# Window attention beside a Fourier mix: sums of v in bursts of four blocks instead of three

## The chip, the cores and the metric

The kernel runs on one core of a Trainium2 chip. A core has a matrix engine (TensorE, PE in the profile, with its weight loads as PEld), a vector engine (VectorE, DVE), an activation engine (ScalarE, ACT), a general engine (GpSimd, POOL) and a queue engine (SyncE, SP) that here only issues transfers. Each engine runs its own instructions in their order and waits on semaphores for the others. The metric is the device time of one execution in microseconds (us); lower is better. Several executions are timed, and one more is recorded by the profiler.

## The reference

Two mixers of the same x (2048 rows of 512) are blended row by row by a gate:

```python
g = _sigmoid((x * gate_w).sum(-1, keepdims=True))
a = einsum("ts,bse->bte", dft_seq_re, x @ dft_hid_re.T) - einsum("ts,bse->bte", dft_seq_im, x @ dft_hid_im.T)
# b: 32 heads of 16, window of 256
scores = jnp.einsum("bhqd,bhkd->bhqk", q, k) * (Dh ** -0.5)
mask = (idx[:, None] - idx[None, :] >= 0) & (idx[:, None] - idx[None, :] < W)
p = _softmax(jnp.where(mask[None, None], scores, -1e9), axis=-1)
b = jnp.einsum("bhqk,bhkd->bhqd", p, v) (heads side by side) @ wo
return g * a + (1 - g) * b
```

a is a discrete Fourier transform written as dense matrix products; b is causal attention in which a row sees itself and the 255 rows before it. B_x is not used: both mixers take A_x.

## The kernel before

**The dense work.** Products in float32 are made of three products of a high and a low part each (TERMS). All dense work of the projections and of the transform (tiles dqk, dv, dab, dc, lines 244, 266, 446; 128x512 each) is one generator, `stream`, that yields after nearly every matmul. The big part is dc: 1536 matmuls, blocks of 48. Its matrices cr and ci come in pieces through the tile raw, and DVE splits each piece in a high part (L80) and a low part (L81).

**The attention.** 2048 rows are 32 blocks of 64; 32 heads are four groups of eight, so there are 128 blocks (N), group after group. A pair is two heads; a group has four pairs (p = 0 to 3). Scores are computed twice. First, `s_pair(n, p)` computes the scores of the 64 queries of block n against up to 320 keys (PE, L325), DVE adds the mask and takes the row minimum (L327), and ACT takes the exponential and the row sum (L330). After each eight blocks `ml_rows` turns minima and sums into rows (a reciprocal and three copies on DVE, two small matmuls L337, three stores through SP), and two visits later `m_ring` sends the minima's rows into the ring buffer of the queries, by a transfer on ACT's queue. Second, LAG = 20 visits behind, `t_pair(k, p)` computes the transposed scores of the 64 keys of block k against up to 320 queries (PE, L388), ACT takes the exponential into the tile pt (L389), and after every second pair POOL zeroes the corners outside the window by four selects (L394, L398; two where the sequence ends). pt has four buffers, a whole block each.

**The sums of v.** `pv(j)` multiplies block j's pt with v (tile vpad, L415): matmuls with 32 columns of weights, so that the four pairs lie beside each other in the array, summed in the PSUM tile o. A tile o holds 512 queries; where a block's window crosses into the next 512, the block's sums are two pieces. When eight blocks have ended, DVE multiplies o with the reciprocal row sums (L425), which a transfer has brought, and the result is stored (o_scr). vpad is made by `v_spread` for four blocks at once (two copies on POOL, L378) from the tile vr that `v_load` fetches; vpad has two buffers and vr one.

**The order.** PE runs in the order written by hand. The loop over visits n does, for each quarter p: one s tile of block n, some matmuls of the stream (`fill`), one T tile of block k = n - 20, another fill. A fill gives 1.5 to 1.8 matmuls on average. The tiles of s, T and ml_rows take turns in four PSUM buffers (pool ps_a, tag st). `make_pad` prepares the stationary operands (two buffers each, on DVE and ACT). At the end of the third quarter of every third visit, PE runs a burst: the sums of the last three blocks, one block after another, and behind it `ml_rows` when a set of eight blocks is due. The other engines' order is set by a planner that simulates the program.

**Behind the loop.** `attention_done` (L640) loads wo. The rest of the stream follows: `wo_prep` reads o_scr back and splits it (tile os), `wo_block` multiplies with wo (L669, 12 matmuls a block), in groups between blocks of dc.

Of the kernel before, what the change touches and what calls it, by code (L numbers as in the profile page):

```python
# [25 lines left out]
LAG = 20  # L26
# [6 lines left out]
def fnet_window_mix(ctx: ExitStack, tc: tile.TileContext, xT, x, wqk, wv, wr, wi, cr, ci, wo, gw, out):  # L33
# [21 lines left out]
    def ld(dst, src):  # L55
        mark("sp", nc.sync.dma_start(dst, src))

    def f(ap):
        return ap.bitcast(F32)
# [7 lines left out]
    @contextmanager  # L67
    def behind(*engines):
        with ExitStack() as es:
            for e in engines:  # L70
                if e in last:
                    es.enter_context(tc.issue_after(last[e]))
            yield
# [98 lines left out]
    def clear_rows(i, ss):  # L172
        nc.gpsimd.memset(f(ring[i][96:128, :, ss * 512:(ss + 1) * 512]), 0.0)
# [7 lines left out]
    def clear_pads():  # L181
        for t in vpad:
            nc.gpsimd.memset(t, 0.0)
        for t in pads[1]:
            nc.gpsimd.memset(f(t[96:128]), 1.0)
            for h in range(2):
                a = t[96:128, :, 64 * h:64 * h + 64]
                nc.vector.tensor_scalar(a, f(a), mrow[96:128, h:h + 1], None, op0=OP.mult)
# [110 lines left out]
    def make_pad(i, n):  # L299
        if not 0 <= n < NG * NB:  # L300
            return
        t = pads[i][n % NPAD]
        b = n % NB
        with behind(*(("act", "dve") if n < NPAD else ())):
            for h in range(2):
                src, dst = f(ring[i][:96, :, b * BQ:(b + 1) * BQ]), t[:96, :, 64 * h:64 * h + 64]
                if i and h:
                    nc.scalar.activation(dst, src, AF.Copy, scale=half[:96, h:h + 1])  # L308
                else:
                    nc.vector.tensor_scalar(dst, src, half[:96, h:h + 1], None, op0=OP.mult)  # L310
        PAD[i, n] = t
# [21 lines left out]
    def ml_rows(u):  # L333
        ml = ML.pop(u)
        nc.vector.reciprocal(ml[:, 1], ml[:, 1])
        pt = ps_a.tile([P, 512], F32, name="s", tag="st")
        nc.tensor.matmul(pt[:64, :P], ml.rearrange("p x c -> p (x c)"), ident, start=True, stop=True)  # L337
        hl = at.tile([32, 2, 2, 64], F32R, name="mhl", bufs=1)
        m = pt[:32, :P].rearrange("c (a r) -> c a r", a=2)
        nc.vector.tensor_scalar(hl[:, :, 0], m, -1.0, None, op0=OP.mult)  # L340
        nc.vector.scalar_tensor_tensor(hl[:, :, 1], m, -1.0, f(hl[:, :, 0]), op0=OP.mult, op1=OP.subtract)
        ld(m_scr[u].rearrange("x p (j r) -> (p j) x r", r=64), f(hl[:]).rearrange("c a h r -> c (a h) r"))
        lt = at.tile([64, P], F32, name="lt", bufs=1)
        nc.vector.tensor_copy(lt[32:64], pt[32:64, :P])
        for a in range(2):
            ls = l_scr[u]
            ld(bass.AP(tensor=ls.tensor, offset=ls.offset + a * 512, ap=[[1024, NP], [64, 8], [1, 64]]),
               lt[32:64, 64 * a:64 * a + 64])

    def m_ring(u):  # L350
        U = u % 4
        with behind("act"):
            nc.scalar.dma_start(f(ring[0][96:100, :, U * 512:(U + 1) * 512]), m_scr[u])
# [17 lines left out]
    def v_spread(n):  # L371
        if n >= NG * NB:
            return
        raw = VR.pop(n)
        v2 = vpad[n // 4 % 2]
        for h in range(2):
            r = slice(64 * h, 64 * h + 64)
            nc.gpsimd.tensor_copy(v2[r, :, :, 16 * h:16 * h + 16], raw[r].rearrange("r j (p d) -> r j p d", d=16))  # L378
        V2[n // 4] = v2

    def t_pair(n, p):
        q0 = n % NB * BQ
        w = min(WIN, S - q0)
        if p == 0:
            PT[n] = at.tile([P, NP, WIN], F32, name="pt", bufs=4)
        pt = PT[n]
        ps = ps_a.tile([P, 512], F32, name="t", tag="st")
        nc.tensor.matmul(ps[:, :w], PAD[1, n][:, p], ring[0][:, p, q0:q0 + w], start=True, stop=True)  # L388
        nc.scalar.activation(pt[:, p, :w], ps[:, :w], AF.Exp, scale=-1.0)  # L389
        if p % 2:  # L390
            ph = slice(p - 1, p + 1)
            for h in (0, 64):
                a = pt[h:h + 64, ph, 0:64]
                nc.gpsimd.affine_select(a, a, pattern=[[0, 2], [1, 64]], compare_op=OP.is_ge, fill=0.0,  # L394
                                        base=0, channel_multiplier=-1)
                if w == WIN:
                    a = pt[h:h + 64, ph, 256:320]
                    nc.gpsimd.affine_select(a, a, pattern=[[0, 2], [-1, 64]], compare_op=OP.is_gt, fill=0.0,  # L398
                                            base=0, channel_multiplier=1)

    def pv(n):
        g, kb = divmod(n, NB)
        v2 = V2[n // 4][:, n % 4]
        pt = PT.pop(n)
        q0 = kb * BQ
        w = min(WIN, S - q0)
        q = q0
        while q < q0 + w:
            sb = q // 512
            e = min(q0 + w, (sb + 1) * 512)  # L410
            first = (g, sb) not in OT
            if first:
                OT[g, sb] = ps_o.tile([P, 512], F32, name="o")
            for p in range(NP):
                nc.tensor.matmul(OT[g, sb][32 * p:32 * p + 32, q - sb * 512:e - sb * 512], v2[:, p],  # L415
                                 pt[:, p, q - q0:e - q0], start=first, stop=kb == 8 * sb + 7,
                                 skip_group_check=True)
            q = e
        if kb % 8 == 7:
            sb = kb // 8  # L420
            ps = OT.pop((g, sb))
            rl = ev.tile([P, 512], F32, name="ev")
            ls = l_scr[g * 4 + sb]
            ld(rl, bass.AP(tensor=ls.tensor, offset=ls.offset, ap=[[512, 2 * NP], [0, 16], [1, 512]]))
            nc.vector.tensor_mul(rl, ps, rl)  # L425
            ld(o_scr[sb][g], rl)
# [251 lines left out]
    def need(key):  # L678
        while key not in have:
            next(stream)  # L680
# [3 lines left out]
    def ring_ahead(n):  # L684
        nonlocal loaded
        while loaded < 16:
            g, ss = divmod(loaded, 4)
            if n >= 32 * g + 8 * ss:
                need(("qk", g, ss))
            if ("qk", g, ss) not in have or n - LAG < 32 * (g - 1) + 8 * ss + 9:  # L690
                break
            with behind(*(("sp",) if g == 0 else ())):
                ring_load(g, ss)
            loaded += 1

    def fill(n):
        nonlocal quota
        rate = FILL_FIRST if n < LAG else FILL_SEQ if "proj" in have else FILL_PROJ
        quota += rate / 2
        while quota >= 1:  # L700
            next(stream, None)
            quota -= 1

    ctx.enter_context(tc.manual_schedule(engines={mybir.EngineType.PE}))
    N = NG * NB
    maxima = sent = 0
    taken = []
# [1 line left out]
    ring_ahead(0)  # L709
    need(("v", 5))  # L710

    for n in range(N + LAG + 2):
        if n in (1, 3, 5):
            for i in range(2):
                clear_rows(1 - i, (n + 1) // 2)
        if n == 7:
            clear_pads()
        k = n - LAG
        ring_ahead(n + 1)
        if -4 <= k < N - 4 and k % 4 == 0:  # L720
            for c in range(2):
                need(("v", (k + 4) % NB // 2 + c))
            with behind(*(("sp",) if k < 4 else ())):
                v_load(k + 4)
        if -4 <= k and k % 4 == 3:
            v_spread(k + 1)
        if n == 0:
            make_pad(0, 0)
        for p in range(NP):
            if n < N:  # L730
                s_pair(n, p)
            fill(n)
            if 0 <= k < N:
                t_pair(k, p)
            if p == 0:
                make_pad(0, n + 1)
                if k >= -1:
                    make_pad(1, k + 1)
            fill(n)
            if p == 2 and sent < maxima and n >= taken[sent] + 2:  # L740
                m_ring(sent)
                sent += 1
            if p == 2 and k % 3 == 0:
                for j in range(k - 3, k):
                    if 0 <= j < N:
                        pv(j)
                if maxima < 16 and n > 8 * maxima + 8:
                    ml_rows(maxima)
                    maxima += 1
                    taken.append(n)  # L750
    attention_done()
    for _ in stream:
        pass
# [44 lines left out]
```

## Time and profile before

| | |
|---|---|
| time, median of 3 runs | 871.07 us (869.48 to 871.13) |
| profiled execution, own time | 873.39 us |
| its span, first to last instruction | 871.3 us |
| PE busy | 860.5 us, 99% |
| DVE busy | 611.3 us, 70% |
| ACT busy | 580.9 us, 67% |
| POOL busy | 384.6 us, 44% |

Busy is the time in which an engine had at least one instruction at work, as a share of the span. Matmuls overlap: the next starts before the one before has ended, and so the distance between two starts, not the duration of one, tells what a matmul costs PE. In a row of the timeline the columns are the start in us, the duration in us, the engine, the line, the operation, the tiles (written <- read), the shape and how many instructions are merged; in brackets the idle time before it and who ended it. In a row of the waits, an engine and the tile it works on stand left of the arrow, and who was waited for right of it, then the total in us, how often, and the longest in us.

### The profile page before, as it was taken

How to read it: one execution, taken by the hardware profiler on the slowest of the kernel's cores; microseconds unless marked ns; L12 is line 12 of the kernel's file. 1: busy time of each engine (PE TensorE's matmuls, PEld its weight loads, DVE VectorE, ACT ScalarE, POOL GpSimd, SP SyncE). 2: the span in 40 equal slices, each digit the busy share in tenths (PEclk: the TensorE clock that was granted, in tenths of full speed). 3: DMA queues.
4: the chain of work that ended last, by engine and by line, in shares of the span. 5: the costliest groups of instructions: out<-in, count | busy, mean ns of one | idle time of the engine just before them, and what ended most of it. 6: DMA issues, size and time to landing. Idle time of an engine off the chain costs nothing.

```text
span 871.3 us, 17146 instructions
## 1 busy us (share of the span) xinstructions
PE 860.5 (99%) x5160; PEld 690.3 (79%) x5160; DVE 611.3 (70%) x1974; ACT 580.9 (67%) x1793; POOL 384.6 (44%) x1067
## 2 busy tenths in 40 slices
PE   8999999999999999999999999999999999999998
PEld 6888778787877778878788887878778787788886
DVE  4588987667878987878787777788876444564431
ACT  4388799888897987878788777877776454111110
POOL 9100054545444756656456566554546665200000
PEclk9999999999999999999999999999999999999999
DMA  6875796464749436644445354599944333485541
GB/s 229 266 226 155 248 262 197 153 214 158 241 158 289 130 105 225 172 130 135 134 131 170 105 163 133 156 349 256 329 148 159 123 118 114 130 263 192 189 145 48
DMA packets 93132, 157.87 MB, mean 181 GB/s; under 512 B 27120, under 2 KB 36080, under 8 KB 93040
## 3 DMA queue, kind: packets, MB, share of 16 engines
q1 hardware_dynamic: 92288, 155.61, 56.5%
q10 hardware_dynamic: 752, 1.18, 0.4%
q8 instruction: 40, 0.66, 0.3%
q14 instruction: 52, 0.43, 0.2%
HBM read 106.69 MB, written 50.07 MB: 180 GB/s over the span
## 4 chain that ended last, share of the span: by engine, by line
PE 92%; DVE 3%; DMA 2%; ACT 1%; issue 1%; SPq 0%; DVEq 0%; ACTq 0%
PE dc L446 40%; PE dab L266 9%; PE s L325 8%; PE o L415 8%; PE dqk L244 8%; PE t L388 8%; PE t L669 5%; PE dv L266 4%; DVE sm L327 1%; PE s L232 1%; DMA raw<-x 1%; ACT sm L330 1%; DMA ring<-qk_scr 1%; PE s L337 1%; DMA pt<-xT 0%
## 5 line engine op out<-in xcount | busy, mean ns | idle before, releaser
L446 PE MATMUL dc<-big,hi 128*128 128x512 f32 x1024 | 355.4, 395 | 0.0
L394 POOL TENSOR_SCALAR_AFFINE_SELECT pt<-pt 64x128 f32<-64x128 f32 x512 | 191.9, 375 | 276.4 <-ACT pt L389 261.2
L330 ACT ACTIVATE sm<-sm,ml 128x320 f32<-128x320 f32 (+4 forms) x512 | 277.3, 543 | 49.4 <-DVE ml L327 48.0
L327 DVE CUSTOM_DVE_ANT_0 sm<-s,mask 128x320 f32<-128x320 f32 (+4 forms) x512 | 230.7, 462 | 82.7 <-PE s L325 62.5
L389 ACT ACTIVATE pt<-t 128x320 f32<-128x320 f32 (+4 forms) x512 | 208.7, 412 | 89.8 <-PE t L388 86.2
L446 PEld LDWEIGHTS dc<-big,hi 128*128 128x128 f32 x1024 | 186.3, 188 | 32.6 <-issue 2.4
L446 PE MATMUL dc<-big,lo 128*128 128x512 f32 x512 | 201.6, 394 | 0.0
L398 POOL TENSOR_SCALAR_AFFINE_SELECT pt<-pt 64x128 f32<-64x128 f32 x448 | 161.9, 361 | 0.1
L325 PE MATMUL s<-ring,pad 128*128 128x320 f32 (+4 forms) x512 | 159.0, 310 | 0.9 <-DVE ml L327 0.5
L388 PE MATMUL t<-ring,pad 128*128 128x320 f32 (+4 forms) x512 | 155.1, 303 | 1.6 <-DVE ml L327 0.9
L310 DVE TENSOR_SCALAR pad<-ring,half 96x256 fp32r<-96x256 f32 x384 | 121.6, 358 | 24.2 <-PE t L388 22.0
L325 PEld LDWEIGHTS s<-ring,pad 128*128 128x128 f32 x512 | 96.0, 188 | 36.6 <-issue 7.4
L388 PEld LDWEIGHTS t<-ring,pad 128*128 128x128 f32 x512 | 96.1, 188 | 21.6 <-DVE ml L327 2.6
L446 PEld LDWEIGHTS dc<-big,lo 128*128 128x128 f32 x512 | 96.3, 188 | 10.6
L81 DVE TENSOR_TENSOR lo<-raw,hi 128x512 fp32r<-128x512 f32 x146 | 99.6, 712 | 1.4 <-PE dc L446 1.3
L330 ACT ACTIVATION_READ_ACCUMULATOR sm<-sm,ml 128x1 f32 x512 | 98.8, 193 | 0.0
L266 PE MATMUL dab<-hi,big 128*128 128x512 f32 x256 | 90.9, 396 | 0.0
L244 PE MATMUL dqk<-big,hi 128*128 128x512 f32 x240 | 86.7, 394 | 0.6 <-DVE hl L86 0.5
L80 DVE CAST hi<-raw 128x512 fp32r<-128x512 f32 x142 | 58.6, 453 | 38.3 <-PE dc L446 37.1
L415 PE MATMUL o<-pt,vpad 128*32 128x320 f32 (+4 forms) x1408 | 73.8, 351 | 0.0
L378 POOL COPY vpad<-vr 64x256 f32<-64x256 f32 x64 | 26.0, 405 | 91.1 <-DMA vr<-v_scr 72.0
L308 ACT ACTIVATE pad<-ring,half 96x256 fp32r<-96x256 f32 x128 | 64.1, 500 | 0.0
(82 smaller groups left out, 780.3 us busy)
## 6 DMA issues: line engine op xcount, KB each, us to landing
qk_scr<-hl SPq DMA_DIRECT2D x32, 512.0 KB
ring<-qk_scr SPq DMA_DIRECT2D x32, 512.0 KB
raw<-cr SPq DMA_DIRECT2D x32, 512.0 KB
raw<-ci SPq DMA_DIRECT2D x32, 512.0 KB
ab_scr<-hl SPq DMA_DIRECT2D x20, 512.0 KB
big<-ab_scr SPq DMA_DIRECT2D x20, 512.0 KB
r_scr<-ev SPq DMA_DIRECT2D x36, 256.0 KB
ev<-r_scr SPq DMA_DIRECT2D x36, 256.0 KB
```

The costliest lines, as they stand in the source:

```text
L244: nc.tensor.matmul(ps, w[a][:, c:c + 128], XT[dk, ss][:, b], start=n == 0, stop=n == 11)
L266: nc.tensor.matmul(ps, XT[dk, ss][:, a, c * 128:(c + 1) * 128], wh[b], start=n == 0, stop=n == 11)
L310: nc.vector.tensor_scalar(dst, src, half[:96, h:h + 1], None, op0=OP.mult)
L325: nc.tensor.matmul(ps[:, :w], PAD[0, n][:, p], ring[1][:, p, k0:k0 + w], start=True, stop=True)
L327: mark("dve", nc.vector.tensor_tensor_reduce(out=sm[:, :w], in0=ps[:, :w], in1=mask[:, WIN - w:], scale=1.0, scalar=3e38, op0=OP.add, op1= ...
L330: mark("act", nc.scalar.activation(sm[:, :w], sm[:, :w], AF.Exp, bias=nm[:, c], scale=-1.0, accum_out=l[:, c]))
L388: nc.tensor.matmul(ps[:, :w], PAD[1, n][:, p], ring[0][:, p, q0:q0 + w], start=True, stop=True)
L389: nc.scalar.activation(pt[:, p, :w], ps[:, :w], AF.Exp, scale=-1.0)
L394: nc.gpsimd.affine_select(a, a, pattern=[[0, 2], [1, 64]], compare_op=OP.is_ge, fill=0.0, base=0, channel_multiplier=-1)
L398: nc.gpsimd.affine_select(a, a, pattern=[[0, 2], [-1, 64]], compare_op=OP.is_gt, fill=0.0, base=0, channel_multiplier=1)
L415: nc.tensor.matmul(OT[g, sb][32 * p:32 * p + 32, q - sb * 512:e - sb * 512], v2[:, p], pt[:, p, q - q0:e - q0], start=first, stop=kb == 8 ...
L446: nc.tensor.matmul(ps, w[a][:, i % 8 * 128:i % 8 * 128 + 128], ab[SC[i]][:, b], start=i == ends[0] and a + b == 0, stop=i == ends[1] and a ...
```

## The change

- The sums of v run for four blocks, in the second quarter of every visit with k divisible by four: behind that quarter's s tile and its first fill. They cover blocks k-4 to k-1. `ml_rows` moves with them.
- In these visits (k > 0) the T tiles of block k are not one per quarter: the first quarter has none, the second has pair 0 (behind the burst), the third pair 1, the fourth pairs 2 and 3, one directly behind the other.
- `v_spread` for the next four blocks runs in visits with k % 4 == 2 instead of 3.
- The loop has one visit fewer: 149 instead of 150. The last burst (blocks 124 to 127) is in the last visit, where before the last one summed two blocks.

```diff
-    for n in range(N + LAG + 2):
+    for n in range(N + LAG + 1):
...
-        if -4 <= k and k % 4 == 3:
-            v_spread(k + 1)
+        if -4 <= k and k % 4 == 2:
+            v_spread(k + 2)
         if n == 0:
             make_pad(0, 0)
+        sums = k > 0 and k % 4 == 0
         for p in range(NP):
             if n < N:
                 s_pair(n, p)
             fill(n)
+            if k % 4 == 0 and p == 1:
+                for j in range(k - 4, k):
+                    if j >= 0:
+                        pv(j)
+                if maxima < 16 and n > 8 * maxima + 8:
+                    ml_rows(maxima)
+                    maxima += 1
+                    taken.append(n)
             if 0 <= k < N:
-                t_pair(k, p)
+                for q in ((), (0,), (1,), (2, 3))[p] if sums else (p,):
+                    t_pair(k, q)
...
-            if p == 2 and k % 3 == 0:
-                for j in range(k - 3, k):
-                    if 0 <= j < N:
-                        pv(j)
-                if maxima < 16 and n > 8 * maxima + 8:
-                    ml_rows(maxima)
-                    maxima += 1
-                    taken.append(n)
```

## The prediction

> **What bounds the kernel now.** I read the page first, then the busy time of the loop's stretch, then the order of TensorE (PE) around a burst of sums, then the waits of PE's weight loads, then POOL's masks, and last the chain of waits behind the loop.
>
> ```profile
> PE 860.5 (99%) x5160; PEld 690.3 (79%) x5160; DVE 611.3 (70%) x1974; ACT 580.9 (67%) x1793; POOL 384.6 (44%) x1067
> ...
> PE 92%; DVE 3%; DMA 2%; ACT 1%; issue 1%; SPq 0%; DVEq 0%; ACTq 0%
> ```
>
> ```profile
> core 0: us, PE busy (x) PEld busy (x) DVE busy (x) ACT busy (x) POOL busy (x), PEclk, DMA share, GB/s
> 123.40:758.90 635.50, 633.15 (x4152) 504.41 (x4151) 470.37 (x1574) 485.37 (x1524) 351.64 (x1000) 1.00 0.55 174
> ```
>
> PE carries 92% of the chain that ended last; in the stretch with bursts it is busy 633.15 of 635.50 us at a clock of 1.00, ACT 485.37 (76%) and DVE 470.37 (74%). So a change helps only if it takes time out of PE's own queue, and it hurts if it makes PE wait. A busy PE hides slots in which matmuls stand further apart than they need to. These show around a burst:
>
> ```profile
> 663.98 0.31 PE L388 MATMUL t<-ring,pad 128*128 128x320 f32 x1
> 664.13 0.39 PE L446 MATMUL dc<-big,hi 128*128 128x512 f32 x1
> 664.45 1.82 PE L415 MATMUL o<-pt,vpad 128*32 128x320 f32 x24
> 666.20 0.50 PE L446 MATMUL dc<-big,hi 128*128 128x512 f32 x1
> 666.53 0.39 PE L446 MATMUL dc<-big,lo 128*128 128x512 f32 x1
> ```
>
> ```profile
> 757.76 0.39 PE L446 MATMUL dc<-big,lo 128*128 128x512 f32 x1
> 757.99 0.39 PE L446 MATMUL dc<-big,hi 128*128 128x512 f32 x1
> 758.30 0.54 PE L415 MATMUL o<-pt,vpad 128*32 128x128 f32 x16
> 758.77 0.50 PE L446 MATMUL dc<-big,hi 128*128 128x512 f32 x1
> 759.11 0.40 PE L446 MATMUL dc<-big,lo 128*128 128x512 f32 x1
> ```
>
> Starts tell the slots: a dc matmul takes 757.99 - 757.76 = 0.23 us, a 320-column tile of T (or s) 664.13 - 663.98 = 0.15. The first burst sums three blocks of 320 columns (960), the second the last two blocks of a group, cut by the end of the sequence to 128 and 64 columns (192). From the dc before to the second dc behind it, the first takes 666.53 - 664.13 = 2.40 us, the second 759.11 - 757.99 = 1.12. So a column costs (2.40 - 1.12)/768 = 1.667 ns (a block 0.53 us), and what stays over is 1.12 - 0.32 - 2 x 0.23 = 0.34 us: a fixed price of each burst, split between the gap ahead of it (0.31 instead of 0.23) and the first matmul behind it (0.34 instead of 0.23).
>
> **The change, part by part.**
>
> *Fewer bursts.* Before, a burst comes at every third visit (k = 3 to 129: 43). After, at every fourth (k = 4 to 128: 32). The columns summed are the same. Eleven fixed prices go: 11 x 0.34 = -3.7 us. All of it lies in PE's queue, on the path. ml_rows stands right behind a burst in both, so its two small matmuls keep their place; one visit fewer in the loop only moves some 14 fill matmuls behind the loop, at the same 0.23.
>
> *The sums visit.* One visit (four quarters, each with an s tile, a T tile and two fills) is read from s tiles ten quarters apart:
>
> ```profile
> 527.18 0.30 PE L325 MATMUL s<-ring,pad 128*128 128x320 f32 x1
> ...
> 538.42 0.31 PE L325 MATMUL s<-ring,pad 128*128 128x320 f32 x1
> ```
>
> A quarter is 11.24/10 = 1.12 us, so a fill is (1.12 - 2 x 0.15)/2 = 0.41. s and T tiles share four PSUM buffers: a tile must be read by DVE (s) or ACT (T) before the fourth one after it starts. Ordinarily that leaves two quarters, 2.24 us. With two T tiles in the last quarter, four handovers per sums visit have three fills and four tiles: 3 x 0.41 + 4 x 0.15 = 1.83 us. Missed handovers in the kernel before:
>
> ```profile
> PEld s L325 <- ACT sm L330: 3.6, 7, 0.5
> PEld s L325 <- DVE ml L327: 3.3, 9, 0.6
> ...
> PEld t L388 <- DVE ml L327: 2.6, 6, 0.8
> ...
> PEld s L325 <- ACT pt L389: 2.0, 4, 0.8
> PEld o L415 <- POOL pt L398: 1.6, 5, 0.4
> ```
>
> The first four rows: 26 misses, 11.5 us, 0.44 each, among 1024 tiles. The change makes 4 x 31 = 124 of them shorter by 0.41. Low end: 0, or a gain of a few misses, because ACT and DVE catch up during a longer burst just ahead. High end: each of the 31 visits misses one, 31 x 0.44 = 13.6. I take one miss, +0.4, near the low end, because the tight handovers come directly behind a burst, when both engines' queues are empty, and 26 in 1024 are missed at all.
>
> *Masks.* The last block's T pairs must be exponentiated (ACT) and masked by four selects (POOL) before the burst reads them. From that block's last T tile to its own products there were a tile, a fill, three quarters and two blocks: 0.56 + 3.36 + 1.07 = 5.0 us. After it is three tiles, four fills and three blocks: 0.45 + 1.64 + 1.60 = 3.7. The time needed, from the tile's start to the end of the fourth select, is mostly below that, but not always:
>
> ```profile
> 278.30 0.31 PE L388 MATMUL t<-ring,pad 128*128 128x320 f32 x1
> ```
>
> ```profile
> 281.83 0.30 POOL L398 TENSOR_SCALAR_AFFINE_SELECT pt<-pt 64x128 f32<-64x128 f32 x1
> ```
>
> ```profile
> 469.56 0.31 PE L388 MATMUL t<-ring,pad 128*128 128x320 f32 x1
> ```
>
> ```profile
> 470.99 1.02 POOL L394 TENSOR_SCALAR_AFFINE_SELECT pt<-pt 64x128 f32<-64x128 f32 x1 [0.88 <-ACT pt L389]
> 471.98 0.29 POOL L398 TENSOR_SCALAR_AFFINE_SELECT pt<-pt 64x128 f32<-64x128 f32 x1
> 472.31 1.32 POOL L394 TENSOR_SCALAR_AFFINE_SELECT pt<-pt 64x128 f32<-64x128 f32 x1
> 473.59 0.29 POOL L398 TENSOR_SCALAR_AFFINE_SELECT pt<-pt 64x128 f32<-64x128 f32 x1
> ```
>
> ```profile
> 573.39 0.31 PE L388 MATMUL t<-ring,pad 128*128 128x320 f32 x1
> ```
>
> ```profile
> 577.23 0.30 POOL L398 TENSOR_SCALAR_AFFINE_SELECT pt<-pt 64x128 f32<-64x128 f32 x1
> ```
>
> Of the 124 blocks behind the start, ten need more than 3.7: the first is the tile at 278.30 (3.83), the last that at 573.39 (4.14), one of the worst that at 469.56 (473.88 - 469.56 = 4.32). Their excess sums to 3.6 us over 124 blocks; 31 of these now stand at the end of a burst: 3.6 x 31/124 = +0.9. Low end 0, high end 31 x 0.62 = 19 (each as late as the tile at 469.56). I take +0.9.
>
> In the late case two selects take 1.02 and 1.32 instead of 0.29, while DVE splits a piece:
>
> ```profile
> 472.20 0.68 DVE L81 TENSOR_TENSOR lo<-raw,hi 128x512 fp32r<-128x512 f32 x1
> ```
>
> [...]
>
> *v_spread, a visit earlier.* Its two copies on POOL move away from the visit whose masks the burst awaits, and their wait for a burst goes:
>
> ```profile
> POOL vpad L378 <- PE o L415: 16.6, 18, 1.7
> ```
>
> After, the buffer's last burst lies two visits back. The 16.6 us were POOL's idle time, on no path; gain 0 to the masks' 0.9, taken as 0. Its load keeps its place and has two visits (9 us) to land instead of three; SP's later loads wait on it no longer than before.
>
> *ml_rows, pv's load and product, m_ring.* DVE now has the product with 1/l and the three ml copies behind one burst in every second sums visit, ahead of the third s tile; SP gets their stores in another order. They stand where DVE has just idled: 0, with the handovers' upper end covering them. The ring rows sent by m_ring are read seven quarters and a burst later (7 x 1.12 + 2.5 = 10.3 us); no PE wait on such a transfer shows before: 0.
>
> *Behind the loop.* The output blocks now start after 64 dc matmuls instead of 92, in five groups instead of four.
>
> ```profile
> 758.84 21.12 PE dc L446 x92
> ```
>
> ```profile
> 773.56 0.68 DVE L81 TENSOR_TENSOR os<-ev,os 128x512 fp32r<-128x512 f32 x1
> ```
>
> Before, the first group's operands were ready at 774.2, 15.4 us into the 21.12. After, there are 64 x 0.23 = 14.7 us. At most 0.7 short, but the first group's three reads now stand on SP ahead of the store of the last burst, so 0.
>
> **Sum.** -3.7 + 0.4 + 0.9 = -2.4 us. The profiled execution took 873.39 us (span 871.3), 2.3 above the median of 871.07; I take the difference to the median: 868.7. What measurement can tell from no change is about 0.2%, 1.7 us.
>
> **Rivals.**
> 1. *Handovers (slower).* For it: ACT and DVE are at 76 and 74%, and the two T tiles arrive together. Against: the misses above are few. At one miss in every second sums visit, 16 x 0.44 = 7.0: -3.7 + 0.9 + 7.0 = +4.2, 875.3. It turns the result slower by 0.2% from (1.7 + 2.8)/0.44 = 10 more misses. Chance 0.14.
> 2. *Masks late (slower).* By the contention in the row at 472.20: if a split meets the last masks in every third burst, 10 x 0.62 = 6.2: -3.7 + 0.4 + 6.2 = +2.9, 874.0. For it: 1.3 us less reserve. Against: v_spread no longer delays that visit. Chance 0.07.
> 3. *Eaten up (same).* Both in part, 3 us together: -0.7, 870.4. Chance 0.18.
> 4. *The whole gain and more (faster).* No new wait, and a few old misses go: -4.5, 866.6. Chance 0.13.
> My forecast (866.9 to 869.3) has 0.48. Faster 0.61, same 0.18, slower 0.21. The range 865.5 to 873.5 leaves out most of the first two rivals; its low end is the saving with some four misses gone.
>
> **What would show it.** 32 bursts, each with the 0.34; PE's time between loop start and end shorter by 11 of them. Waits of PEld on POOL around 1 us in total say the masks were sized right, 6 or more say rival 2; the four handover rows near 12 us in total say the forecast, near 19 rival 1. A gap ahead of the first output group would show the stage behind the loop wrong. A fixed price that grows with the blocks in a burst would make the first term wrong.

## The result: slower by 0.7%

The changed kernel takes 876.23 us (median of 6 runs, 873.9 to 878.95), the kernel before beside it 870.11 us (6 runs, 868.44 to 871.13). The ratio is 1.0071 with a 95% interval of 1.0048 to 1.0095. The prediction was 868.7; its range ended at 873.5. The profiled execution took 877.35 us with a span of 875.5 us. The six runs of the changed kernel differ in PE's mean granted clock: the run of 873.9 has 1.000, those of 877.35 to 878.95 have 0.996 or 0.997.

The page of the changed kernel, its busy time and the engines' shares of the chain that ended last:

```profile
PE 860.7 (98%) x5160; PEld 693.1 (79%) x5160; DVE 610.7 (70%) x1974; ACT 582.3 (67%) x1793; POOL 386.5 (44%) x1067
...
PE 76%; DMA 4%; ACT 2%; DVE 2%; issue 1%; POOL 1%; ACTq 0%; SPq 0%; DVEq 0%; POOLq 0%
```

The windows view of the changed kernel over the same stretch of 635.5 us as in the prediction:

```profile
123.40:758.90 635.50, 626.50 (x4105) 501.07 (x4098) 467.87 (x1561) 484.41 (x1515) 350.82 (x991) 1.00 0.55 173
```

PE carried 92% of the chain before and carries 76% after; DMA doubled to 4%. The two shares of PE don't compare as they stand: both are shares of the whole span, and the chain of the changed kernel is followed back only to 122.99 us, over 86% of it; of that part PE has 88%. The stretch is the better measure. There PE stands still for 635.50 - 626.50 = 9.0 us, where it was 2.35. So the kernel lost time in waits of PE, and more of the chain runs through transfers.

**The bursts.** A burst of four blocks in PE's timeline of the changed kernel (start, duration):

```profile
666.02 0.39 PE L446 MATMUL dc<-big,lo 128*128 128x512 f32 x1
666.25 0.61 PE L446 MATMUL dc<-big,hi 128*128 128x512 f32 x2
666.80 2.39 PE L415 MATMUL o<-pt,vpad 128*32 128x320 f32 x32
669.11 0.42 PE L388 MATMUL t<-ring,pad 128*128 128x320 f32 x1
669.37 0.40 PE L446 MATMUL dc<-big,lo 128*128 128x512 f32 x1
```

From 666.02 to 669.37 are 3.35 us: three dc slots (0.69), one T slot (0.15), 1280 columns at 1.667 ns (2.13), and 0.38 over, with the rounding of six slots in it. The same reckoning over all 32 bursts, late masks left out, gives 0.35 to 0.36 for each of the 18 without `ml_rows`. The 14 with `ml_rows` stand at 0.73 each, because its two small matmuls are counted in. That makes 16.8 us for all; the 43 bursts before, again 14 of them with `ml_rows`, took 20.5. The difference is -3.7 us, as predicted.

**Late masks.** PE's timeline around the burst at 122.28, then POOL's and DVE's at the same place:

```profile
122.28 2.35 PE L415 MATMUL o<-pt,vpad 128*32 128x320 f32 x28
125.01 0.73 PE L415 MATMUL o<-pt,vpad 128*32 128x320 f32 x4 [0.39 <-POOL pt L398]
```

```profile
122.23 0.77 POOL L394 TENSOR_SCALAR_AFFINE_SELECT pt<-pt 64x128 f32<-64x128 f32 x1 [0.85 <-ACT pt L389]
122.95 1.05 POOL L398 TENSOR_SCALAR_AFFINE_SELECT pt<-pt 64x128 f32<-64x128 f32 x1
124.05 0.65 POOL L394 TENSOR_SCALAR_AFFINE_SELECT pt<-pt 64x128 f32<-64x128 f32 x1
124.66 0.29 POOL L398 TENSOR_SCALAR_AFFINE_SELECT pt<-pt 64x128 f32<-64x128 f32 x1
```

```profile
122.82 0.72 DVE L81 TENSOR_TENSOR lo<-raw,hi 128x512 fp32r<-128x512 f32 x1
...
123.87 0.68 DVE L81 TENSOR_TENSOR lo<-raw,hi 128x512 fp32r<-128x512 f32 x1
```

The four selects end at 124.95, and the burst's last matmuls start at 125.01. Three of the four take 0.65 to 1.05 us instead of 0.29, with DVE's splits beside them; the burst is 1.1 us longer than its columns and its fixed price. Five of the 32 bursts are late, by 1.1, 0.94, 0.58, 0.14 and 0.07 us: 2.8 us in all (0.1 before).

**A transfer that PE waits for.** PE, SP and DVE of the changed kernel around 396 us, and the piece of the chain between them:

```profile
390.89 2.38 PE L415 MATMUL o<-pt,vpad 128*32 128x256 f32 x64
...
395.65 0.39 PE L446 MATMUL dc<-big,hi 128*128 128x512 f32 x1
399.49 1.07 PE L388 MATMUL t<-ring,pad 128*128 128x320 f32 x2 [3.46 <-DVE lt L344]
400.36 0.63 PE L446 MATMUL dc<-big,hi 128*128 128x512 f32 x1
```

```profile
389.07 1.19 SPq L56 DMA_DIRECT2D ring<-qk_scr  x2
390.30 0.64 SPq L56 DMA_DIRECT2D ev<-l_scr  x1
```

```profile
390.30 7.42 DMA ev<-l_scr
```

```profile
397.84 0.69 DVE L425 TENSOR_TENSOR ev<-o,ev 128x512 f32<-128x512 f32 x1 [5.08 <-DMA ev<-l_scr]
398.45 0.27 DVE L340 TENSOR_SCALAR mhl<-s 32x128 fp32r<-32x128 f32 x1
398.75 0.28 DVE L341 SCALAR_TENSOR_TENSOR mhl<-s,mhl 32x128 fp32r<-32x128 f32 x1
399.06 0.28 DVE L344 COPY lt<-s 32x128 f32<-32x128 f32 x1
```

The burst from 390.89 ended a set of eight blocks. The planner put the product with the row sums (L425) directly behind it on DVE, ahead of the three copies of `ml_rows` (L340 to L344) and of the next score tiles. The row sums' transfer was issued at 390.30, only 0.6 us ahead of the burst and behind two ring transfers (512 and 256 KB), and landed after 7.42 us. DVE waited 5.08 us, the copies behind it held the PSUM buffer that T's next tile needed, and PE stood for 3.6 us (399.49 - 395.65 less one slot).

In the kernel before, the same product also stood right behind the sums of its set, in the burst at 401.69, and did not wait (PE, SP and DVE):

```profile
401.69 1.83 PE L415 MATMUL o<-pt,vpad 128*32 128x128 f32 x40
```

```profile
394.75 0.63 SPq L56 DMA_DIRECT2D ev<-l_scr  x1
```

```profile
402.66 0.68 DVE L425 TENSOR_TENSOR ev<-o,ev 128x512 f32<-128x512 f32 x1
```

There the transfer was issued 401.69 - 394.75 = 6.9 us ahead of the burst. So the product kept its place behind its sums, and the burst came earlier: this set ends with block 55, which was summed in visit k = 57 and is now summed in k = 56. The transfer did not come earlier with it. In both kernels SP issues it behind the two ring transfers, for which its queue had waited for PE (2.4 us before, 4.2 after, by the profile). Of the 16 sets this is the only one with so short a lead: the others have 6.7 us or more in the changed kernel, and the least before was 5.0. The copies of `ml_rows` stood one burst ahead of the product before (at 385.87) and stand behind the same burst now.

On the row sums DVE waited once before too, for another set (the waits of the kernel before):

```profile
DVE ev L425 <- DMA ev<-l_scr: 3.1, 1, 3.1
```

No stop of PE over 0.4 us stands behind it. The transfer was issued at 565.95, 5.0 us ahead of its burst (570.93), PE was in the burst until 572.69, and the product started at 573.95, 1.3 us behind it. In the changed kernel it started 4.6 us behind the burst (393.20).

Behind this stop PE ran at a lower clock. The windows view of the changed kernel for the stop, the stretch behind it and the next (the third column from the end is PE's clock):

```profile
395.60:399.50 3.90, 0.44 (x4) 0.13 (x2) 1.56 (x5) 0.08 (x1) 1.07 (x4) 1.00 0.57 161
399.50:403.30 3.80, 3.75 (x10) 3.06 (x11) 2.07 (x9) 2.64 (x9) 1.07 (x4) 0.55 0.36 102
403.30:407.00 3.70, 3.70 (x20) 3.18 (x20) 2.19 (x9) 2.98 (x11) 1.39 (x4) 1.00 0.05 8
```

At 0.55 for 3.8 us, 3.8 x 0.45 = 1.7 us more are lost. (0.55 is a mean: from 399.90 to 403.20 the view gives 0.50.) The stop costs 5.3 us.

**A second transfer.** ACT's timeline at 618 us, and the chain there:

```profile
618.90 0.64 ACTq L353 DMA_DIRECT2D ring<-m_scr  x1
619.59 0.44 ACT L389 ACTIVATE pt<-t 128x320 f32<-128x320 f32 x1 [2.43 <-DMA big<-ab_scr]
```

```profile
611.25 7.63 DMA big<-ab_scr
```

ACT's queue stands at the issue of `m_ring`'s transfer, which waits until a transfer of the dense work has landed; T's exponentials stand behind it, and PE stops for 1.7 us.

The groups of waits of the changed kernel, those that the prediction named and the new ones:

```profile
POOL vpad L378 <- PE o L415: 55.5, 29, 2.8
...
DVE ev L425 <- DMA ev<-l_scr: 5.1, 1, 5.1
PEld t L388 <- ACT pt L389: 4.5, 6, 1.9
PEld o L415 <- POOL pt L398: 4.4, 9, 1.0
...
PEld s L325 <- DVE ml L327: 3.6, 7, 1.3
PE t L388 <- DVE lt L344: 3.5, 1, 3.5
ACT pt L389 <- DMA big<-ab_scr: 2.4, 1, 2.4
PE t L388 <- ACT pt L389: 2.3, 3, 1.6
PEld s L325 <- ACT pt L389: 2.2, 6, 0.5
...
PEld t L388 <- DVE ml L327: 1.0, 3, 0.5
```

**The account.** I took each distance between two starts on PE, less the ordinary slot of its shape (0.229 us for a dense matmul, 0.147 for a tile of 320 columns), and summed what was over. Outside the bursts, between 100 and 760 us, that is 14.9 us before and 23.7 after: +8.7, of which the stop at 395.65 with its slow clock is 5.3, the stop at 618 is 1.7, and stops of 1.0 us at 276 and 0.6 at 577 make up most of the rest. A slot taken 1 ns smaller adds 1.8 us to both sums and leaves the difference. With -3.7 for the fixed price, +2.7 for the masks and -3.4 for the stretch before 100 us (7.3 before, 3.9 after) it comes to +4.3; the spans differ by 875.5 - 871.3 = 4.2. The last term is not the change's: the profiled execution of before was itself slow at its start (its clock was 0.50 from 8.60 to 12.00 us) and 3.3 us above the median of the six runs beside the change (873.39 against 870.11). The medians differ by 6.1.

### The profile page after: what moved, and what is told of

Read it like the earlier page. It is cut to its first block, busy times and chain, and to the rows that moved or that the text cites. A ratio compares the mean times of both kernels' runs of the same rounds, so it can differ in the third digit from the quotient of the medians.

```text
span 875.5 us, 17135 instructions
## 1 busy us (share of the span) xinstructions
PE 860.7 (98%) x5160; PEld 693.1 (79%) x5160; DVE 610.7 (70%) x1974; ACT 582.3 (67%) x1793; POOL 386.5 (44%) x1067
## 4 chain that ended last, share of the span: by engine, by line
PE 76%; DMA 4%; ACT 2%; DVE 2%; issue 1%; POOL 1%; ACTq 0%; SPq 0%; DVEq 0%; POOLq 0%
PE dc L446 38%; PE t L388 8%; PE dab L266 7%; PE o L415 7%; PE s L325 6%; PE t L669 5%; PE dqk L244 4%; ACT sm L330 1%; DMA raw<-x 1%; DMA big<-ab_scr 1%; DMA ev<-l_scr 1%; DMA ev<-r_scr 1%; ACT pt L389 1%; DMA o_scr<-ev 1%; PE s L337 0%
## 5 line engine op out<-in xcount | busy, mean ns | idle before, releaser
L398 POOL TENSOR_SCALAR_AFFINE_SELECT pt<-pt 64x128 f32<-64x128 f32 x448 | 165.1, 368 | 0.1
L325 PE MATMUL s<-ring,pad 128*128 128x320 f32 (+4 forms) x512 | 155.1, 303 | 1.9 <-DVE ml L327 1.4
L446 PEld LDWEIGHTS dc<-big,lo 128*128 128x128 f32 x512 | 96.6, 189 | 11.3
L81 DVE TENSOR_TENSOR lo<-raw,hi 128x512 fp32r<-128x512 f32 x146 | 99.1, 707 | 0.0
L80 DVE CAST hi<-raw 128x512 fp32r<-128x512 f32 x142 | 58.3, 451 | 51.6 <-PE dc L446 46.2
```

Source lines behind the costliest of these rows:

```text
L325: nc.tensor.matmul(ps[:, :w], PAD[0, n][:, p], ring[1][:, p, k0:k0 + w], start=True, stop=True)
L446: nc.tensor.matmul(ps, w[a][:, i % 8 * 128:i % 8 * 128 + 128], ab[SC[i]][:, b], start=i == ends[0] and a + b == 0, stop=i == ends[1] and a ...
```

## The experiments

Three theories. *Transfers*: the gain of the fewer bursts is there, and a queue whose head waits for a transfer (DVE at L425, ACT at L353) takes more than that. *Masks*: the shorter reserve of the last block takes it. *Handovers*: the two T tiles in one quarter take it. All ratios are to the kernel before, timed beside each kernel; its median was 869.7 to 871.5 us. The change itself was timed in the result alone, so a difference to it is a difference of two ratios, uncertain by some 0.26% or 2.3 us. In some of the kernels the lines are shifted by one or more.

**1. Bursts of two blocks** (from the kernel before): measures the fixed price by itself.

```diff
-            if p == 2 and k % 3 == 0:
-                for j in range(k - 3, k):
+            if p == 2 and k % 2 == 0:
+                for j in range(k - 2, k):
```

> The kernel before, with bursts of two blocks at every second visit, 64 bursts instead of 43, at the same place in the visit. If each burst has a fixed price of 0.34 to 0.36 us on TensorE: 21 x 0.35 = 7.4 us slower, 877 to 878. If the price grows with the blocks in a burst, so that fewer bursts save nothing: within 1.5 us of 870.

Measured 879.91 us, 1.0117 (1.0095 to 1.0139). 21 more bursts cost 27.6 - 20.5 = 7.1 us in fixed price: 0.34 each, so the price does not grow with the blocks. The rest came from the same two sources as in the change: masks late in bursts 2.9 us, and one stop of 2.4 us at 400.84 where DVE waited 4.5 us at L425.

**2. Without the far corner's selects** (the change; the select L398 is left out, so the far corner of the window is not zeroed): takes the masks' load off POOL.

```diff
-                if w == WIN:
+                if w < 0:
                     a = pt[h:h + 64, ph, 256:320]
```

> The changed kernel without the second select on GpSimd (L398, the far corner of the window is not zeroed, so that part of the mask is left out); GpSimd has about half the work and the last masks ahead of a burst come some 0.6 us sooner. If late masks cost what the trace shows (2.9 us of stops inside five bursts), the time falls by 2 to 3.5 us, to about 873, and the waits of the weight loads on GpSimd (4.8 us) go to under 1. If late masks are beside the point (theory A alone), it stays within 1 us of 876.2.

Measured 872.08 us, 1.0025 (1.0014 to 1.0036): 0.46% or 4.0 us less than the change. Late masks fell from 2.8 to 0.2 us, and the stop at L353 from 1.7 to 0.4. The waits of PEld on POOL stayed at 4.1 us, where I had expected under 1. The waits of this kernel keep the row sums:

```profile
DVE ev L425 <- DMA ev<-l_scr: 4.9, 1, 4.9
...
PE t L388 <- DVE lt L344: 3.3, 1, 3.3
```

The masks are a real loss; the largest stop stands without them.

**3. Without row sums** (the change; L425 becomes a copy and the transfer goes, so the division by the softmax's sums is left out).

```diff
-            ld(rl, bass.AP(tensor=ls.tensor, offset=ls.offset, ...))
-            nc.vector.tensor_mul(rl, ps, rl)
+            nc.vector.tensor_copy(rl, ps)
```

> The changed kernel with a copy in place of the product L425, and without the transfer of the row sums: the division by the softmax's sums is left out. The wait for this transfer is taken away with nothing fetched earlier instead. Theory (this wait is the stop of 3.6 us and the slow clock behind it): 4.5 to 6 us faster than the changed kernel, 870.5 to 871.5. Rival: 876 within 1.5 us.

Measured 871.36 us, 0.9998 (0.9985 to 1.0011): 0.73% or 6.3 us less than the change. The stop at 396 is gone. Masks (3.3 us) stay, and ACT's queue at L353 now makes PE stop twice, for 1.8 and 2.0 us. So the wait for the row sums is the largest single loss. The edit also takes 16 transfers of 256 KB off the DMA queues, and no run separates that from the wait; in experiment 4, where the transfers stay, this stop goes as well.

**4. Row sums fetched early**, in the change and in the kernel before: the transfer is issued four visits before its product.

```diff
+    def rl_load(u):
+        RL[u] = ev.tile([P, 512], F32, name="ev")
+        ls = l_scr[u]
+        ld(RL[u], bass.AP(tensor=ls.tensor, offset=ls.offset, ...))
...
         ring_ahead(n + 1)
+        if 0 <= k < N and k % 8 == 4:
+            rl_load(k // 8)
```

> The changed kernel, with the row sums for the product L425 fetched four visits earlier (the transfer is issued in visits with k % 8 == 4 instead of together with the burst that ends the eight blocks). Theory A (the changed kernel loses its gain because VectorE stands at L425, right behind a burst, waiting for this transfer, with the maxima's copies and the score tiles queued behind it): the wait of VectorE at L425 for the transfer (5.1 us in the changed kernel) is gone, no stop of TensorE of 3.6 us and no slow clock behind it; the time falls by 4 to 6 us, to 870 to 872. Rival B (the time goes into many small waits for late masks and late score tiles, and the one long stop is an accident of the profiled execution): the time stays within 1.5 us of the changed kernel's 876.2.

> The kernel before, with the same earlier fetch of the row sums (visits with k % 8 == 4). Theory A: before, the product L425 stood later on VectorE and its one wait of 3.1 us for the transfer stopped nobody, so the time stays at 870, within 1.5 us. Rival (the early fetch is a gain of its own, whatever the bursts): faster by 3 us or more.

In the change: 873.2 us, 1.0037 (1.0025 to 1.005), 0.34% or 3.0 us less than the change as it was, where I had expected 4 to 6. The stop at 396 is gone, but ACT's queue now stops longer at 612, because the transfer that its issue waits for is now the row sums' (timeline of ACT):

```profile
615.15 0.64 ACTq L353 DMA_DIRECT2D ring<-m_scr  x1
615.84 0.44 ACT L389 ACTIVATE pt<-t 128x320 f32<-128x320 f32 x1 [4.17 <-DMA ev<-l_scr]
```

PE stood for 3.5 us there, where it had been 1.7, and behind the stop two dc slots took 0.85 us instead of 0.46 (from 616.74). In the kernel before: 873.1 us, 1.0035 (1.0021 to 1.0048), where I had expected no change. A stop of 3.0 us appeared at 276 us, where DVE waited 3.8 us for x (the chain):

```profile
268.67 8.72 DMA raw<-x
```

So the same edit, harmless on paper, costs the kernel before 0.35%. In these two profiles, moving one transfer changed which other one is late.

**5. m_ring's transfer on SP's queue**, in the change, and with the early row sums.

```diff
-        with behind("act"):
-            nc.scalar.dma_start(f(ring[0][96:100, :, U * 512:(U + 1) * 512]), m_scr[u])
+        ld(f(ring[0][96:100, :, U * 512:(U + 1) * 512]), m_scr[u])
```

> The changed kernel with m_ring's transfer issued by SyncE instead of ScalarE. Theory: ScalarE stood at this transfer's issue (2.4 us at 616 to 619 us in the changed kernel, 4.2 us in the kernel with the early row sums) until another, unrelated 512 KB transfer had landed, and the T tiles' exponentials stood behind it. Then the stop at 618 us is gone, the one at 396 us (VectorE at L425) stays: 1.5 to 2.5 us faster than the changed kernel, about 874. Rival (the exponentials were late for another reason): the stop stays and the time is 876 within 1 us.

> The changed kernel with both: row sums fetched four visits earlier and m_ring issued by SyncE. If the two late transfers are the loss and the early fetch only moved the second stop (1.7 us grew to 3.5 us and a slow clock behind it): 868.5 to 870, that is 4 us less than with the early row sums alone. If the stops only move to another engine's queue each time: 872 to 874.

Alone: ratio 1.0046 (1.0026 to 1.0067), median 876.95. That is 2.2 us under the change by the ratios, as I had expected, but the two intervals overlap. ACT's stop at 618 is gone, DVE's at L425 stays (4.7 us). Both: 875.03 us, 1.0032 (1.0018 to 1.0047), against an expectation of 868.5 to 870. Neither old stop is left, but a new one of 3.8 us stands at 584, where DVE's cast (L80) waits for a piece of ci (the chain):

```profile
575.20 11.79 DMA raw<-ci
```

**6. T earlier in the visit before the burst**, alone and with the other edits: in visits with k % 4 == 3 T's pairs 2 and 3 both stand in the third quarter, so that the last masks have a quarter more. The expectations call the kernel with all three edits e10.

```diff
-                for q in ((), (0,), (1,), (2, 3))[p] if sums else (p,):
+                for q in ((), (0,), (1,), (2, 3))[p] if sums else ((0,), (1,), (2, 3), ())[p] if k % 4 == 3 else (p,):
```

> The change with one thing added: in the last visit of each four (k%4==3) T's pairs 2 and 3 both stand in the third quarter and none in the fourth, so that ACT's exponentials and POOL's selects of the last block have a quarter more before the burst. Row sums and m_ring's transfer stay where the change has them. If the masks that come late in the burst (2.8 us in the change's profile) are a loss of their own, this kernel is 2 to 2.5 us under the change (about 874 beside 876.2 for the change and 870.1 for before), with PEld o <- POOL pt under 1.5 us in all, and the long stop at L425 (3.6 us) stands as it was. If the masks only filled a time that another wait would have taken, it is within 0.5 us of the change.

> The kernel before it in this batch (T's last two pairs of k%4==3 a quarter earlier), with m_ring's transfer issued by SyncE, not by ScalarE; the row sums' load stays in pv. The queue theory says: ScalarE's stop at L353 is gone (1.7 us in the change), the stop of VectorE at L425 stays or moves to another late transfer; about 872 to 874. If the row sums' load had to stand early for the gain of e10, it is at 873 or above; if ring on SyncE and T earlier make up e10's gain by themselves, it is at 870 to 871.

> As the run before, and in the visits just ahead of a burst (k % 4 == 3) the T tiles of pairs 2 and 3 both run in the third quarter and none in the fourth. The last masks get one quarter (1.12 us) more. If late masks cost 2.8 us inside the bursts: 2 to 2.8 us less than the run before, about 867, which would be faster than the kernel before. If the denser T tiles make the score tiles late instead: no less than the run before, and the four rows of missed handovers grow by 2 us or more.

Alone it takes 878.57 us, 1.0084 (1.0067 to 1.0101), no faster than the change, against an expected gain of 2 to 2.5. Late masks did fall, from 2.8 to 1.4 us, but the row sums now come late twice, at 394 (2.7 us) and 562 (2.4 us), and the stop at L353 grew to 3.4. At the second place the changed kernel had issued the transfer 6.8 us ahead of its burst (560.53), and the product stood 8.8 us behind the issue (SP and DVE, the change):

```profile
553.78 0.64 SPq L56 DMA_DIRECT2D ev<-l_scr  x1
```

```profile
562.60 0.69 DVE L425 TENSOR_TENSOR ev<-o,ev 128x512 f32<-128x512 f32 x1 [0.39 <-PE o L415]
```

and this kernel issues it behind the ring's transfers, 1.7 us ahead of its burst (557.21). It landed after 7.25 us, with the product right behind (the chain):

```profile
555.55 7.25 DMA ev<-l_scr
...
562.92 0.69 DVE ev L425
```

With m_ring on SP as well: 875.86 us, 1.0055 (1.0039 to 1.0071); the two late row sums stay, stops of 2.9 and 3.1 us; behind the one at 394 the clock was 0.50 from 397.40 to 403.20. That was 2 us above its expectation, which had reckoned with one stop.

With row sums early, m_ring on SP and T earlier together: 870.35 us, 0.9979 (0.9967 to 0.9991). This kernel computes everything and beats both, the kernel before by 0.2% or 1.8 us; I had expected about 867. One stop of 2.6 us is left at 579, behind a piece of ci that landed 11.32 us after its issue.

**7. Row sums two visits later than in that kernel** (k % 8 == 6).

> e10_and_t_earlier with the row sums' load two visits later (k%8==6, still two visits ahead of its use). In e10 what was left was one stop of 2.6 us at 579 behind a transfer of ci that landed 11.3 us after its issue. If that stop comes from where the row sums' load stands in SyncE's queue, it goes or moves here, and the kernel is between 867 and 870; if it comes from the load of ci alone, the stop stands at the same place with 2 to 3 us, and the time is that of e10 (870.4) within 0.5.

Measured 869.52 us, 0.9987 (0.9972 to 1.0002): not told apart from that kernel, nor from the kernel before. The stop at 579 shrank from 2.6 to 0.9 us, and one of 1.9 us came at 624, again DVE's cast waiting for ci. In these two profiles, then, the place of the row sums' load in SP's queue changes which piece of ci is late. Late masks are 0.3 us.

**8. All three losses out** (the change; no row sums, m_ring on SP, T earlier; the division by the softmax's sums is left out).

> The change without its three found losses: no load of row sums and L425 a copy (the division by the softmax's row sums is left out), m_ring's transfer on SyncE, T's last two pairs of k%4==3 a quarter earlier. If these three are the whole of what ate the gain, the time is the prediction's sum without the masks, 866 to 867.5 (870.1 less 11 bursts of 0.34, and row sums that the kernel before too waits 0 for on TensorE). If something else in the change costs too, or a further transfer comes late, it is at 869 or above and the trace shows one more long stop.

Measured 865.55 us, 0.9941 (0.9926 to 0.9957), just under the 866 to 867.5 expected. The windows view of this kernel over the usual stretch:

```profile
123.40:758.90 635.50, 632.91 (x4159) 509.00 (x4148) 476.53 (x1574) 483.88 (x1515) 348.18 (x989) 1.00 0.53 170
```

PE stands for 2.6 us in 635.5, as in the kernel before (2.35). Outside bursts 14.4 us are over (14.9 before), late masks are 0.4, the fixed price is 16.7. With the waits out, the kernel is 0.59% or 5.1 us (3.7 to 6.4) faster than the kernel before, of which the fewer bursts are 3.7. Where the other 1.4 comes from is open. The kernel before was not run without its own row sums, so a part may be the 16 transfers that are gone here; the interval holds 3.7 at its end.

## Why the prediction was wrong, step by step

- **Fewer bursts, -3.7**: right, to the tenth, and the price does not depend on the number of blocks (0.34 for each further burst of two, 0.34 with three, 0.35 to 0.36 with four).
- **"ml_rows, pv's load and product, m_ring. They stand where DVE has just idled: 0"**: this is the step that failed. It put the term at nothing by counting the instructions, and left out the transfer that the product waits for. The product stands right behind its sums in both kernels. With the burst moved ahead, the issue of the row sums came 0.6 us ahead of it instead of 6.9, and the landing took 7.42: one stop of 3.6 us and 1.7 us of slow clock behind it. Experiment 3 (6.3 us less without the row sums) and experiment 4 (the stop gone with an early fetch) show it. The same paragraph's "no PE wait on such a transfer shows before: 0" for m_ring was wrong by the 1.7 us of ACT's stop; it asked who reads the rows, and the stop stood at the issue. That the trace of before showed no such stop was no bound: there every issue stood 5.0 us or more ahead of its burst. It struck one set of the 16. I had the row that warned, DVE's one wait of 3.1 us on the row sums in the kernel before, and did not ask how much later than its burst the product would start once the burst moved.
- **Masks, +0.9**: masks did come late in bursts, and the size was off: 2.8 us. I had spread the excess of ten late blocks evenly over all 124; in the event five of 32 bursts were late, two of them by about 1 us. The largest, at 122.28, was the first burst, whose blocks my count had left out. Nor is a stretched select rare: in the changed kernel 98 of the 130 selects that overlap a split into the low part (L81) take over 0.4 us, 45 of the 92 that overlap a cast (L80) do, and 15 of the other 738. The prediction showed the split alone; its select of 1.02 us at 470.99 ran beside casts (from 471.12). The sign that I named, waits of PEld on POOL of about 1 us or of 6 and more, measures badly: the change has 4.4 + 0.4 us there, and the kernel of experiment 7, with late masks of 0.3 us, has 5.0. There most of the waits of weight loads cost PE nothing; the starts tell.
- **Handovers, +0.4**: of the four rows named, the first is gone and the others sum to 3.6 + 1.0 + 2.2 = 6.8 us, 11.5 for all four before. A row that I had not named, T's weight loads on ACT, grew from 1.5 to 4.5. With it the sum is 13.0 before and 11.3 after, and parts of that belong to the long stops. The first rival did not happen.
- **v_spread, "their wait for a burst goes"**: false in fact, 0 in effect. The wait grew from 16.6 to 55.5 us, because the copies now wait for the burst more often (29 times, 18 before); POOL idles there, and no row of the waits shows PE held up by it.
- **Behind the loop, 0**: right. The dc matmuls behind the loop run into the output blocks without a gap.
- **Against which time**: the profiled execution of before was 2.3 us above the median of its three runs, and 1.7 us of that is the clock of 0.50 for 3.4 us near its start; I took the sum to the median, which stands.

None of the four rivals had a transfer that comes late behind a moved burst. The second (masks, 874.0) had a part of the cause.

## What to carry to other kernels

When a step moves, list for each transfer that its instructions read the time from its issue to the moment at which the reader is otherwise ready, before and after. Set it against the longest landing of its kind under the load at that place (here 7.0 to 8.0 us for the row sums, up to 9.05 for another transfer of 256 KB, up to 11.8 for 512 KB). A lead under that can be a wait, however little the reader itself costs: row sums issued 0.6 us ahead of their burst made DVE wait 5.1 us in the change, those issued 5.0 ahead 3.1 in the kernel before, and those issued 6.7 us or more ahead none in either. Then ask what stands behind the reader in its queue: DVE's wait of 3.1 us in the kernel before left no stop of PE, and that of 5.1 us cost 5.3, because a buffer that PE needed was behind it. Where a planner places transfers, a saving in one queue can shift others. Here only several small edits together brought the change below the kernel before, by 0.2% at most among the kernels that compute everything; each of them alone stayed within 0.4% of the change.

## What the runs showed of the hardware that I had not expected

A short stop of PE can have a price behind it. After the stop of 3.6 us in the change the clock was 0.55 for 3.8 us. The windows view of the kernel with T earlier (experiment 6, alone) shows the same behind a stop of 2.4 us:

```profile
560.00:564.50 4.50, 2.36 (x11) 1.71 (x11) 1.48 (x5) 0.88 (x2) 1.55 (x6) 1.00 0.67 192
564.50:568.50 4.00, 3.88 (x11) 3.09 (x12) 2.15 (x9) 3.32 (x10) 1.07 (x4) 0.58 0.36 104
```

In that slow stretch two dc matmuls start 0.43 us apart (566.46 and 566.89), where the ordinary slot is 0.23. After its other late row sums, a stop of 2.7 us at 394, the clock was 0.62 for 4.5 us, and after the stop of 2.6 us in the kernel with all three edits 0.57 for 4 us. After stops of 1.7 (the change, at 618), 1.9 (experiment 7, at 624) and 1.8 and 2.0 us (experiment 3) it stayed at 1.00, and after the 2.4 us in the kernel with bursts of two as well. So 2.4 us between two starts beyond the ordinary slot had a slow clock behind them in one run and not in another; how long a stop must be for it, these runs don't show.

How long a transfer takes from issue to landing differs. Where something waited for them, the row sums (256 KB) took 7.0 to 8.0 us, a piece of x (256 KB) 6.53 in the kernel before, 8.72 in that kernel with the early row sums and 9.05 in the change, and ci's pieces (512 KB) 8.64 in the kernel of experiment 7, 11.32 and 11.79 in those of experiments 6 and 5.

Selects on POOL took longer beside some work of DVE in the changed kernel: at 122.95, beside the split at 122.82, one took 1.05 us instead of 0.29. Beside casts too many were long: 45 of the 92 that overlap one took over 0.4 us, against 15 of the 738 that overlap neither a cast nor a split.
